# Routed attention with a tanh-shrink MLP: the up-projection of batch 0's second half as seven products of quarters

## Chip, cores, metric

One core of one Trainium2 chip. The metric is device time in microseconds, the median of several runs; a profile is one execution of its own, with a span a little below the run's time.

## The reference

```python
# q, k, v: (4, 8, 768, 64) f32; centroids: (8, 16, 64); w_in: (512, 2048); w_out: (2048, 512)
q_assign = argmax(einsum('bhsd,hcd->bhsc', q_n, c_n), -1)     # *_n: normalized rows
k_assign = argmax(einsum('bhsd,hcd->bhsc', k_n, c_n), -1)
mask = q_assign[:, :, :, None] == k_assign[:, :, None, :]
scores = where(mask, scale * (q @ k.T), -1e9)
attn = softmax(scores); x = attn @ v                          # then (B,H,S,D) -> (B*S, 512)
h = x @ w_in
out = (h - tanh(h)) @ w_out                                   # (3072, 512)
```

A query attends only to keys with its own cluster. The second part is a two-layer MLP over 3072 tokens, 768 for each of the 4 batches.

## The kernel before

**Attention in steps.** Heads go in pairs: 16 pairs, 4 to a batch, numbered n = 0 to 15. A pair is worked in two halves of 384 queries, a half in three steps (NS) of two key blocks: 96 steps in all. HALF is 12 steps. Batch 0 takes all first halves of its pairs (steps 0 to 11), then all second halves (12 to 23); from pair 4 on, a pair's two halves follow each other. The loop over `steps` (its index is `at`) writes out the order on every engine by hand (`manual_schedule`); engines run their lists in that order.

In round `at` the loop issues the scores of step at+1 (`begin`, L451: TensorE matmuls into two PSUM tiles, exponentials by ScalarE), and the values of step `at` (`value`, L505). The masks of step at+1 (`select`, L483: VectorE, exponentials where query and key cluster agree) go into a list `todo`, as do the stages of the next pair's preparation: `turn` transposes (pt, L332), `similar` (sim, L351), `route` (four VectorE operations that find each row's best cluster, L364 to L377), `publish` and `spread` (the codes go through DRAM and come back as a row, L402 and L409). GpSimd adds the masked weights up (L492, L496).

**The MLP between.** A finished batch's MLP is cut into items, and the items due in a round (`now`, chosen by weights that stand for their TensorE time) are placed between the scores and values of that round. Each item calls `between` once or twice, and that issues the next share of `todo`: so masks and items' own evacuations alternate on VectorE. Batch 0's first half is filled into steps 12 to 23, its second half into steps 24 to 47, both by `plain_items`: 16 `up` items (h, L676: 8 matmuls of 384 columns each, tanh on ScalarE, subtraction on VectorE, L683) and 12 `project` items (o, L692). Batches 1 to 3 go by `strassen_items`: seven products of quarters in place of eight, with `up_product` (pu, L871, adds on VectorE L859, tanh L864, subtraction on GpSimd L866) and `down_product` (pd, L922). All three kinds of items share three PSUM buffers (tag "f") with sim, pr, pq and den.

**Factors.** The Strassen weights are sums of quarters of w_in and w_out. `up_maker` and `down_maker` list the work: sums on VectorE (made, L773) into one of three buffers, and writes to DRAM on the SP queue (L737: 28 of 256 KB for w_in; L756: 14 of 512 KB for w_out). These items are handed out in rounds 24 to 45. `fetch_factors` (L795, SP) brings the factors of one block back into one of three stream buffers; `open_stream` gives w_in's place to these buffers in round 39. `right_factors` (L832, VectorE) makes the differences of the quarters of xT, partly in place.

xT of a half is divided by the softmax sums by `divide` (L653, L656) for the last pair of a batch, by `scale` (L638) for others, whose sums take a way through DRAM (`total_both`, `compact`, `invert`, `spread_out`).

Rounds are told by their times in the trace: the scores of steps 21, 22, 23 and 24 begin at 159.8, 170.2, 180.4 and 190.2 us, the first `up` of the second half at 205.8, its first `project` at 290.0, batch 1's first product at 374.6.

Of the kernel before, what the change touches and what calls it, by code (L numbers as in the profile page):

```python
# [39 lines left out]
P = 128  # L40
# [18 lines left out]
def kernel(  # L59
# [119 lines left out]
    def fast():  # L179
# [178 lines left out]
        def route(n: int):  # L358

            t = sims.pop(n)  # L360
            ps = ps_f.tile([P, TB], F32, name="pr", tag="f")
            for j in range(HCH):
                c = slice(j * P, (j + 1) * P)
                nc.tensor.transpose(out=ps[:, c], in_=t[:, c], identity=ident)  # L364
            G = HCH * 8
            pr = ps.rearrange("p (g c) -> p g c", c=C)
            shape = [P, G, C]
            places = down.unsqueeze(1).to_broadcast(shape)
            mx = rtp.tile([P, G], F32, name="mx")
            nc.vector.reduce_max(out=mx, in_=pr, axis=AX.X)  # L370
            top = rtp.tile(shape, F32, name="top")
            nc.vector.tensor_tensor(  # L372
                out=top, in0=pr, in1=mx.unsqueeze(2).to_broadcast(shape), op=ALU.is_ge
            )
            nc.vector.tensor_tensor(out=top, in0=top, in1=places, op=ALU.mult)
            code = codes[n] = codep.tile([P, 2, 2, 2, HCH], F32, name="code")
            nc.vector.reduce_max(  # L377
                out=code.rearrange("p i a h j -> p j (i a h)"),
                in_=top.rearrange("p (j g) c -> p j g c", j=HCH), axis=AX.X,
            )  # L380
# [238 lines left out]
        def spread_out(n: int, half: int):  # L619
            back = lists.pop((n, half))  # L620
            if joined(n):
                pool = late_pools.get("den", sump)
                dens[n, 1] = pool.tile([P, TB], F32, name="den")
                for i in range(2):
                    for h in range(2):
                        nc.sync.dma_start(
                            dens[n, i][h * D : h * D + D], back[i, h : h + 1].to_broadcast([D, TB])
                        )
                return
# [35 lines left out]
        def plain_items(half: int):  # L665
# [39 lines left out]
            if half == 0:  # L705

                order = [(s, i) for i in range(NQ4) for s in range(2)] + order[2 * NQ4 :]
            return [(2.6, 1, lambda between, f=f: up(f, between)) for f in sequence] + [
                (3.4, 1, lambda between, s=s, i=i: project(s, i, between)) for s, i in order
            ]  # L710
# [75 lines left out]
        def fetch_factors(n: int):  # L786

            if n < (B - 1) * PER:
                i = n % PER
                t = streams[n] = late_pools["stream"].tile([P, HF, HM], F32, name="stream")  # L790
# [5 lines left out]

        late_pools, diffs = {}, {}

        def open_stream():
# [3 lines left out]
            )  # L803
            late_pools["den"] = cx.enter_context(
                tc.tile_pool(name="den_late", bufs=1, side="right", reuse_waits="tile")
            )
            for n in range(2):
                fetch_factors(n)

        def open_late():  # L810
            first.close()
            for name, bufs in (
                ("diff", 1), ("u", 2), ("s", 2), ("th", 2), ("g", 1), ("left", 1), ("du", 1),
                ("c", 4), ("raw", 2),
            ):
# [4 lines left out]
            late_pools["S1"] = late_pools["left"].tile([P, HF, TB], F32, name="S1")  # L820

        def right_factors(b: int, c: int):

            if c == 0:
                diffs[b] = late_pools["diff"].tile([P, 3, CH, TB], F32, name="diff")
            d = diffs[b]
            x, y = xT[b * HP + c], xT[b * HP + CH + c]
            for out, u, w in (
# [4 lines left out]

        def strassen_items(b: int):
            base = (b - 1) * PER

            held = {}
            G, left1 = late_pools["G"], late_pools["S1"]

            def up_product(i: int, k_: int, between):  # L840
                which = PRODUCTS[k_]
                x = [xT[b * HP + c] for c in range(CD)]
                d = diffs[b]
                right = {
                    1: [x[c][:, 0] for c in range(CH)], 2: [x[CH + c][:, 0] for c in range(CH)],
                    3: [x[CH + c][:, 1] for c in range(CH)], 4: [d[:, 2, c] for c in range(CH)],
                    5: [d[:, 0, c] for c in range(CH)], 6: [d[:, 1, c] for c in range(CH)],
                    7: [x[c][:, 1] for c in range(CH)],
                }[which]
                if k_ == 0:  # L850
                    held[i] = (
                        late_pools["s"].tile([P, TB], F32, name="s"),
                        late_pools["u"].tile([P, 2, TB], F32, name="u"),
                    )
                s, u = held[i]
                g = G[:, i]

                def add(out, x, y):
                    nc.vector.tensor_tensor(out=out, in0=x, in1=y, op=ALU.add)  # L859

                def shrink(f: int, halves_=slice(0, 2)):
                    t = g[:, f, halves_]
                    th = late_pools["th"].tile([P, 2, TB], F32, name="th")[:, halves_]
                    nc.scalar.activation(out=th, in_=t, func=ACT.Tanh)  # L864
                    t, th = (x.rearrange("p a n -> p (a n)") for x in (t, th))
                    nc.gpsimd.tensor_tensor(out=t, in0=t, in1=th, op=ALU.subtract)  # L866

                ps = ps_f.tile([P, TB], F32, name="pu", tag="f")
                for c in range(CH):
# [7 lines left out]
                elif which == 2:  # L877
                    add(g[:, 0, 0], ps, s)
                    if i == HF - 1:
                        shrink(0, slice(0, 1))  # L880
                elif which == 6:
# [4 lines left out]
                elif which == 4:  # L886
                    add(g[:, 1, 0], ps, u[:, 1])
                elif which == 5:
                    add(u[:, 0], ps, u[:, 0])
                    add(g[:, 1, 1], ps, u[:, 1])  # L890
                    shrink(1)
                else:
                    add(g[:, 0, 1], ps, u[:, 0])

                    shrink(0, slice(1 if i == HF - 1 else 0, 2))
                between()
                if k_ == len(PRODUCTS) - 1:

                    nc.gpsimd.tensor_tensor(out=left1[:, i], in0=g[:, 0, 1], in1=g[:, 1, 1], op=ALU.add)
                    nc.gpsimd.tensor_tensor(  # L900
                        out=g[:, 0, 1], in0=g[:, 0, 0], in1=g[:, 0, 1], op=ALU.subtract
                    )
                    streams.pop(base + i)

            us = {}

            def down_product(k_: int, j: int, between):
# [51 lines left out]

            return [  # L960
                (1.3, 1, lambda between, i=i, k_=k_: up_product(i, k_, between))
                for i in range(HF) for k_ in range(len(PRODUCTS))
            ] + [
                (3.4, 2, lambda between, k_=k_, j=j: down_product(k_, j, between))
# [10 lines left out]
        def before(n: int):  # L975
# [9 lines left out]
            yield lambda: similar(n)  # L985
            yield lambda: route(n)
            yield lambda: publish(n)
# [5 lines left out]

        ready = {}
        for n in range(2, len(pairs)):
# [66 lines left out]
        keep_warm(2)  # L1062
        route(0)
        turn(1, 0, nc.scalar)
        turn(1, 1, nc.scalar)
# [11 lines left out]
        round_piece(rounding.pop(0))  # L1077
        route(1)
        begin(steps[0])
        round_piece(rounding.pop(0))  # L1080
# [22 lines left out]
        for at, (n, half, s) in enumerate(steps):  # L1103
            b, p = pairs[n]
            following = steps[at + 1] if at + 1 < len(steps) else None
            if at == 4 * HALF:
                open_late()
            if at == 4 * HALF - 9:
                open_stream()
            if at in fills:  # L1110
                fill, over = fills[at][0](), fills[at][1]
                whole, spent, since = sum(it[0] for it in fill), 0.0, at
            if at == 2 * HALF:
                makers = [it for i in range(2) for it in up_maker(i)]
                makers += [it for i in range(2) for it in down_maker(i)]
            now = []
# [65 lines left out]
            if following:  # L1182
                todo += [lambda i=i: select(*following[:2], 2 * following[2] + i) for i in range(2)]

                if half == 1 and s == NS - 1 and joined(n):
                    todo.insert(1, lambda n=n: total_both(n))
            todo += [stages[i] for i in (5, 3, 4, 2) if i in stages]
            todo += late
            late = []
# [16 lines left out]

            light = [i for i in range(at, 4 * HALF - 2) if i % 3 and i % 6 != 1]
            if makers and at in light:
# [3 lines left out]
            if "raw" in late_pools:  # L1212
                todo += [check_done, check_done, check_on, check_on]
                if p == HP - 1 and half == 1 and s == NS - 2:
                    todo += [lambda b=b, c=c: right_factors(b, c) for c in range(CH - 1)]
            slots = max(sum(it[1] for it in now), 1)
            place = iter(range(slots))
            turned_at = max(slots - 1 - now[-1][1], 0) if now else 0
# [19 lines left out]
        tail = strassen_items(B - 1)  # L1238

        PRS = len(PRODUCTS)  # L1240
        tail = tail[:2] + tail[PRS : PRS + 2] + tail[2:PRS] + tail[PRS + 2 :]
        for it in tail[:2]:
# [217 lines left out]
```

## Time and profile before

| | us |
|---|---|
| runs | 982.23, 983.19, 982.80 |
| median | 982.8 |
| span of the profiled execution | 981.3 |
| its mean granted TensorE clock | 0.999 |

The profile names a group of instructions by line, engine, operation and tiles (out<-in), then gives shapes, count, busy time, mean duration of one in ns, and the engine's idle time ahead of them with what ended it. In a timeline a row is start, duration, engine, line, operation, shapes and count. In the table by stretch the columns are the stretch, its length, busy time and count for TensorE, its weight loads, VectorE, ScalarE and GpSimd, the clock, the share of DMA and GB/s. In the list of waits: total us, times, longest. DMA-issuing instructions on SP are shown as SPq. Two groups of the kinds that the change moves around:

```profile
L871 PE MATMUL pu<-xT,stream 128*64 128x384 f32 x768 | 134.9, 488 | 0.7 <-DVE top L372 0.7
L683 DVE TENSOR_TENSOR g<-h,th 128x384 f32<-128x384 f32 x32 | 17.6, 551 | 26.4 <-ACT th L681 26.3
```

The first is batches 1 to 3's products on values that are not differences, the second the plain up-projection's evacuation.

### The profile page before, as it was taken

How to read it: one execution, taken by the hardware profiler on the slowest of the kernel's cores; microseconds unless marked ns; L12 is line 12 of the kernel's file. 1: busy time of each engine (PE TensorE's matmuls, PEld its weight loads, DVE VectorE, ACT ScalarE, POOL GpSimd, SP SyncE). 2: the span in 40 equal slices, each digit the busy share in tenths (PEclk: the TensorE clock that was granted, in tenths of full speed). 3: DMA queues.
4: the chain of work that ended last, by engine and by line, in shares of the span. 5: the costliest groups of instructions: out<-in, count | busy, mean ns of one | idle time of the engine just before them, and what ended most of it. 6: DMA issues, size and time to landing. Idle time of an engine off the chain costs nothing.

```text
span 981.3 us, 16550 instructions
## 1 busy us (share of the span) xinstructions
PE 972.3 (99%) x6456; PEld 461.1 (47%) x6456; DVE 534.5 (54%) x1010; ACT 316.6 (32%) x484; POOL 498.8 (51%) x347
## 2 busy tenths in 40 slices
PE   9999999999999999999999999999999999999997
PEld 5433443344443334444455555444455555444664
DVE  6458656447566577647655457655754436543011
ACT  5586554233332333233422222333242121222000
POOL 1026334445445454677686345666688445466600
PEclk9999999999999999999999999999999999999999
DMA  7664452024665633463544646345343132233221
GB/s 201 185 192 142 147 143 94 30 73 132 156 204 166 173 116 110 148 195 99 186 151 158 189 136 201 110 151 149 123 159 135 62 118 95 83 113 129 104 103 35
DMA packets 113385, 132.47 MB, mean 135 GB/s; under 512 B 60388, under 2 KB 93076, under 8 KB 110612
## 3 DMA queue, kind: packets, MB, share of 16 engines
q1 hardware_dynamic: 106916, 109.81, 36.5%
q0 software_dynamic: 6240, 21.50, 6.3%
q8 instruction: 53, 0.87, 0.4%
q14 instruction: 32, 0.26, 0.1%
q10 hardware_dynamic: 144, 0.03, 0.0%
HBM read 110.14 MB, written 21.17 MB: 134 GB/s over the span
## 4 chain that ended last, share of the span: by engine, by line
PE 97%; DVE 1%; DMA 0%; issue 0%; SPq 0%; ACT 0%; DVEq 0%
PE pd L922 22%; PE pu L871 22%; PE sc L451 14%; PE av L505 14%; PE o L692 8%; PE h L676 8%; PE pt L332 2%; PE sim L351 1%; PE den L520 1%; PE warm L302 1%; PE den L566 1%; PE den L539 1%; PE pr L364 1%; DVE e L483 1%; DMA row<-q_codes 0%; PE pq L396 0%
## 5 line engine op out<-in xcount | busy, mean ns | idle before, releaser
L496 POOL TENSOR_TENSOR sum<-sum,e 128x768 f32<-128x768 f32 x112 | 207.2, 1850 | 98.0 <-DVE e L483 92.1
L483 DVE SCALAR_TENSOR_TENSOR e<-row,code,sc 128x384 f32<-128x384 bf16 x336 | 186.2, 607 | 104.2 <-ACT sc L473 89.9
L473 ACT ACTIVATE sc<-sc 128x768 f32<-128x768 f32 x168 | 125.9, 792 | 215.8 <-PE sc L451 206.4
L922 PE MATMUL pd<-stream,G 128*64 128x256 f32 x1728 | 191.5, 379 | 0.0
L922 PEld LDWEIGHTS pd<-stream,G 128*64 128x64 f32 x1728 | 123.7, 137 | 67.0 <-issue 7.7
L451 PE MATMUL sc<-t,t 64*128 64x384 f32 x768 | 150.2, 509 | 0.4 <-ACT e L473 0.3
L505 PE MATMUL av<-e,vals 128*64 128x384 f32 x768 | 145.6, 498 | 0.4 <-DVE e L483 0.4
L871 PE MATMUL pu<-xT,stream 128*64 128x384 f32 x768 | 134.9, 488 | 0.7 <-DVE top L372 0.7
L866 POOL TENSOR_TENSOR G<-G,th 128x768 f32<-128x768 f32 (+1 forms) x51 | 87.3, 1723 | 93.9 <-ACT th L864 93.9
L871 PE MATMUL pu<-diff,stream 128*64 128x384 f32 x576 | 102.3, 488 | 0.0
L451 PEld LDWEIGHTS sc<-t,t 64*128 64x128 f32 x768 | 65.8, 186 | 75.0 <-issue 40.8
L492 POOL TENSOR_TENSOR sum<-e 128x768 f32<-128x768 f32 x28 | 55.5, 1983 | 77.9 <-DVE e L483 42.2
L871 PEld LDWEIGHTS pu<-xT,stream 128*64 128x64 f32 x768 | 54.1, 137 | 69.6 <-issue 61.9
L864 ACT ACTIVATE th<-G 128x768 f32<-128x768 f32 (+1 forms) x51 | 40.9, 806 | 141.2 <-DVE G L859 141.2
L692 PE MATMUL o<-w_out,g 128*64 128x512 f32 x384 | 86.4, 594 | 0.0
L505 PEld LDWEIGHTS av<-e,vals 128*64 128x64 f32 x768 | 47.5, 136 | 82.5 <-issue 79.7
L676 PE MATMUL h<-xT,w_in 128*64 128x384 f32 x512 | 86.3, 487 | 0.0
L871 PEld LDWEIGHTS pu<-diff,stream 128*64 128x64 f32 x576 | 40.4, 137 | 51.0 <-issue 44.7
L859 DVE TENSOR_TENSOR G<-pu,u 128x384 f32<-128x384 f32 x72 | 39.8, 553 | 43.5 <-PE pu L871 43.5
L676 PEld LDWEIGHTS h<-xT,w_in 128*64 128x64 f32 x512 | 36.4, 137 | 46.2 <-issue 45.1
L933 DVE SCALAR_TENSOR_TENSOR c<-pd,du 128x256 f32<-128x256 f32 x36 | 15.2, 421 | 67.0 <-PE pd L922 67.0
L692 PEld LDWEIGHTS o<-w_out,g 128*64 128x64 f32 x384 | 27.0, 137 | 50.1 <-issue 49.4
(131 smaller groups left out, 828.9 us busy)
## 6 DMA issues: line engine op xcount, KB each, us to landing
stream<-up_factors SPq DMA_DIRECT2D x24, 896.0 KB
stream<-down_factors SPq DMA_DIRECT2D x21, 1024.0 KB
raw<-in_moe_w_in_dram POOLq DMA_DIRECT2D x16, 512.0 KB, 4.7
raw<-in_moe_w_out_dram POOLq DMA_DIRECT2D x16, 512.0 KB, 3.9
again<-in_moe_w_in_dram SPq DMA_DIRECT2D x32, 256.0 KB
again<-in_moe_w_out_dram SPq DMA_DIRECT2D x32, 256.0 KB
x<-in_q_dram SPq DMA_DIRECT2D x32, 192.0 KB
x<-in_k_dram SPq DMA_DIRECT2D x32, 192.0 KB
```

The costliest lines, as they stand in the source:

```text
L451: nc.tensor.matmul(sc[i][:, h, 0:TB], lhsT=turned[n, 1][r].rearrange("p a n -> p (a n)")[:, j * P : (j + 1) * P], rhs=turned[n, 0][r, half ...
L473: nc.scalar.activation(out=out, in_=sc[i][:, :, 0:TB], func=ACT.Exp, scale=SCALE)
L483: nc.vector.scalar_tensor_tensor(out=e[:, h], in0=rows[n, half][:, h], scalar=codes[n][:, 1, j // HCH, h, j % HCH : j % HCH + 1], in1=sc[: ...
L492: nc.gpsimd.tensor_tensor(out=s, in0=pair[0], in1=pair[1], op=ALU.add)
L496: nc.gpsimd.tensor_tensor(out=s, in0=s, in1=pair[i], op=ALU.add)
L505: nc.tensor.matmul(avs[n, half][h * D : h * D + D], lhsT=vals[n][:, h, j], rhs=e[i][:, h], start=(j == 0), stop=(j == NCH - 1),)
L676: nc.tensor.matmul(h[r], lhsT=w_in[i][:, c, o * P : (o + 1) * P][:, r], rhs=xT[c][:, half], start=(c == 0), stop=(c == CD - 1),)
L692: nc.tensor.matmul(acc[sub][r], lhsT=gs[f % HF][:, f // HF, sub * P : (sub + 1) * P][:, r], rhs=w_out[f // FQ][:, f % FQ], start=(f == seq ...
L864: nc.scalar.activation(out=th, in_=t, func=ACT.Tanh)
L866: nc.gpsimd.tensor_tensor(out=t, in0=t, in1=th, op=ALU.subtract)
L871: nc.tensor.matmul(ps[r], lhsT=streams[base + i][:, c, k_, r], rhs=right[c], start=(c == 0), stop=(c == CH - 1),)
L922: nc.tensor.matmul(ps[r], lhsT=left(i)[:, r], rhs=t[:, i], start=(i == 0), stop=(i == HF - 1))
```

## The change

The second half of batch 0 takes its up-projection by `up_items`, which is the old `up_product` loop with the batch's places passed in: 8 blocks of 7 products, on quarters of 192 columns for batch 0 (the half's 384 queries are cut in two). Products 1 and 2 of the first two blocks come first. The projections stay `project`.

- The up factors are made in rounds 20 to 22 and the stream is opened in round 23, its first two loads being issued there. The factors are fetched 8 blocks more than before. The down factors are made in rounds 36 to 46.
- The differences are made at the start of round 24's items, ahead of the masks of step 25.
- In rounds 24 to 35 the masks of the next step are issued ahead of the round's items (with `total_both` between them where it is due); `route` is cut in two there, and its last two VectorE operations (`route_on`) come later in the list.
- The weights of items: 0.65 for a product, 3.0 for a projection of this half.
- Scratch for s and u, and for one denominators' tile, is taken from the pool of turned q and k.

```diff
+        def route_on(n: int):
+            top = tops.pop(n)
             nc.vector.tensor_tensor(out=top, in0=top, in1=places, op=ALU.mult)
             code = codes[n] = codep.tile([P, 2, 2, 2, HCH], F32, name="code")
             nc.vector.reduce_max(
...
+            ups = [(2.6, 1, lambda between, f=f: up(f, between)) for f in sequence]
+            if half == 1:
+                ups = half_up_items(gs)
+            return ups + [
+                (3.4 if half == 0 else 3.0, 1, lambda between, s=s, i=i: project(s, i, between)) for s, i in order
             ]
...
-                i = n % PER
+                i = n + HF if n < 0 else n % PER
...
+            half_pools["diff"] = mid.enter_context(
+                tc.tile_pool(name="diff_mid", bufs=1, side="right", reuse_waits="tile")
             )
             for n in range(2):
-                fetch_factors(n)
+                fetch_factors(n - HF)
...
+        def columns(b: int, c: int):
+            return xT[b * HP + c] if b else xT[c][:, 1].rearrange("p (a n) -> p a n", a=2)
...
-            x, y = xT[b * HP + c], xT[b * HP + CH + c]
+            x, y = columns(b, c), columns(b, CH + c)
...
-        def strassen_items(b: int):
-            base = (b - 1) * PER
+        def up_items(b: int, base: int, quarter, shrink, done):
             held = {}
+            width = TB if b else TB // 2
...
-                ps = ps_f.tile([P, TB], F32, name="pu", tag="f")
+                ps = ps_f.tile([P, TB], F32, name="pu", tag="f")[:, 0:width]
...
+        def start_without(items):
+            n = len(PRODUCTS)
+            return items[:2] + items[n : n + 2] + items[2:n] + items[n + 2 :]
+
+        def half_up_items(gs):
+            W = TB // 2
+            def quarter(i: int, f: int, t: int):
+                if i not in gs:
+                    gs[i] = gp.tile([P, 2, TB], F32, name="g")
+                return gs[i][:, f, t * W : (t + 1) * W]
+            def shrink(i: int, f: int, parts):
+                cols = slice(parts.start * W, parts.stop * W)
+                t = gs[i][:, f, cols]
+                th = thp.tile([P, TB], F32, name="th")[:, cols]
+                nc.scalar.activation(out=th, in_=t, func=ACT.Tanh)
+                nc.gpsimd.tensor_tensor(out=t, in0=t, in1=th, op=ALU.subtract)
+            return start_without(up_items(0, -HF, quarter, shrink, lambda i: None))
...
-            if at == 4 * HALF - 9:
+            if at == 2 * HALF - 1:
                 open_stream()
...
+            if at == 2 * HALF - 4:
+                makers = [it for i in range(2) for it in up_maker(i)]
             if at == 2 * HALF:
-                makers = [it for i in range(2) for it in up_maker(i)]
-                makers += [it for i in range(2) for it in down_maker(i)]
+                makers = [it for i in range(2) for it in down_maker(i)]
...
-            light = [i for i in range(at, 4 * HALF - 2) if i % 3 and i % 6 != 1]
+            light = [i for i in range(max(at, 3 * HALF), 4 * HALF - 1) if i % 6 != 1]
+            if at < 2 * HALF - 1:
+                light = list(range(at, 2 * HALF - 1))
...
+            if at == 2 * HALF:
+                for c in range(CH):
+                    right_factors(0, c)
+            if 2 * HALF <= at < 3 * HALF:
+                masks = 3 if half == 1 and s == NS - 1 else 2
+                for it in todo[:masks]:
+                    it()
+                todo = todo[masks:]
```

## The prediction

> **What bounds the kernel now.** I read the busy table and the waits of TensorE first, because they decide whether removed matmuls are removed time; then the timeline around the place of the edit; then the DMA by stretch. The page's first part, its clock row, and the three longest entries of TensorE's wait list:
>
> ```profile
> PE 972.3 (99%) x6456; PEld 461.1 (47%) x6456; DVE 534.5 (54%) x1010; ACT 316.6 (32%) x484; POOL 498.8 (51%) x347
> ...
> PEclk9999999999999999999999999999999999999999
> ```
> ```profile
> PE warm L302 <- DVE inverses L231: 1.3, 1, 1.3
> PE pu L871 <- DVE top L372: 0.7, 2, 0.3
> PE av L505 <- DVE e L483: 0.4, 1, 0.4
> ```
>
> TensorE is busy from end to end at full clock, and all its listed waits come to 2.9 us. So every microsecond of matmul taken out in the middle is a microsecond of span, as long as no wait is put in its place. The question is then twofold: what the products cost on TensorE, and whether anything that feeds them comes late.
>
> The matmul's price must be read from starts, since 486 ns records overlap. From the timeline of TensorE (start, duration, instructions at the end; each f32 matmul is two instructions):
>
> ```profile
> 377.24 1.46 PE L871 MATMUL pu<-diff,stream 128*64 128x384 f32 x8
> 378.53 1.46 PE L871 MATMUL pu<-xT,stream 128*64 128x384 f32 x8
> ...
> 491.27 7.08 PE L922 MATMUL pd<-stream,G 128*64 128x256 f32 x64
> 498.27 1.56 PE L451 MATMUL sc<-t,t 64*128 64x384 f32 x8
> ...
> 501.10 3.62 PE L922 MATMUL pd<-stream,G 128*64 128x256 f32 x32
> 504.66 0.55 PE L364 MATMUL pr<-ident,simt 128*128 128x128 f32 x3
> ```
>
> Eight instructions of 384 columns take 378.53 - 377.24 = 1.29 us, 161 ns each. For 256 columns, 64 take 7.00 and 32 take 3.56, so 32 more cost 3.44, 107.5 ns each. That is 0.42 ns a column plus about 1 ns, and a change of product inside a run costs nothing. 192 columns should take 81.3 ns (estimate from these two).
>
> **What the Trainium skill says.** "TensorE: Matmul & The Clock Gate", section Back-to-back issue gap, gives N/2.4 + 2.5 ns warm: 82.5 ns for 192 columns, close to my 81.3. It warns that loads of weights also pace small matmuls; its section on LDWEIGHTS prices a load by its columns, P/1.2 ns, 53 ns for 64. The trace has no 192-column matmul; it shows a pair of 64-column loads lying over each other in about 140 ns, while a pair of 192-column matmuls would take 163. "DMA: Bandwidth & Descriptors", section Queues, rings and completion order, says descriptors of one issuing engine are consumed in ring order on each DMA engine: the new stream loads stand behind the factor writes of the same queue. "GPSIMD Engine Reference", section Specifications, says POOL contends with VectorE instructions of two SBUF inputs. The trace agrees: scaling xT (two SBUF inputs) has a mean of 1420 ns at 384 columns, while the adds of L859, with one input in PSUM, stay at 553 to 555.
>
> **The change part by part.**
>
> ```profile
> L676 PE MATMUL h<-xT,w_in 128*64 128x384 f32 x512 | 86.3, 487 | 0.0
> L866 POOL TENSOR_TENSOR G<-G,th 128x384 f32<-128x384 f32 x6 | 6.0, 1004 | 4.8 <-ACT th L864 4.8
> L496 POOL TENSOR_TENSOR sum<-sum,e 128x768 f32<-128x768 f32 x112 | 207.2, 1850 | 98.0 <-DVE e L483 92.1
> ```
>
> Removed: half of L676, 256 instructions x 161.3 ns = 41.3 us of TensorE. Added: 8 blocks x 7 products x 2 row blocks x 2 column halves = 224 matmuls, 448 instructions x 81.3 ns = 36.4 us. Difference -4.9 us. The number of runs, each with some 0.1 us at its edge, stays about the same (12 steps with one run each), so I take 0 there. The 12 output projections keep their matmuls; only their place shifts by fractions of a step.
>
> The differences: 8 VectorE operations of 192 columns. 128 columns cost 294 ns and 384 cost 553, so about 360 ns, 2.9 us in all; with contention up to 1.2 us more. They follow the last scaling of xT:
>
> ```profile
> 198.16 0.56 DVE L656 TENSOR_TENSOR xT<-xT,den 128x384 f32<-128x384 f32 x1
> 206.16 2.19 DVE L483 SCALAR_TENSOR_TENSOR e<-row,code,sc 128x384 f32<-128x384 bf16 x4 [7.45 <-ACT sc L473]
> ```
>
> VectorE idles 7.45 us there; the differences fit. The first product that needs one is the fifth, and it starts at about 205.8 + 4 x 0.65 = 208.4. Cost 0.
>
> Evacuation: 64 adds of 192 columns (0.36 us) instead of 16 subtractions (0.55): 23 against 8.8 us, over twelve steps of about 6.2 us, next to 2.2 us of masks a step. VectorE has 54 of 79 us busy in this stretch before (205.8 to 284.6), partly the sums for the factors, which move away. ScalarE gains 8 short copies. GpSimd gains 17 subtractions of 384 columns at 1.0 us beside 24 sums at 1.85: 61 of about 74 us. The sums have two steps until their weight buffer is wanted again, so I put this at 0.
>
> What does reach TensorE is the order masks, then adds. In a step that begins at 0, scores end at 1.5, values at 2.8, products follow every 0.65. In the trace masks start 1.91 us after the scores (208.55 to 210.46) and four take 2.2: the first add ends at about 4.45. Three PSUM buffers make the fourth product, at 4.8, wait for it: a margin of 0.3. It fails where route_on's two operations come first (one step, some 0.3 us) and where a route's transposes share the buffers with five products (one step, 0.4). I charge 0.8 us, between 0 and 5 (0.4 in each step).
>
> The factors and their transfer. In the trace the 28 writes of 256 KB are issued from 201.8 to 280.0; now they lie in the three steps from about 167, and the loads of blocks 0 and 1 are issued behind them on SP. Four such writes, then the DMA over time:
>
> ```profile
> 223.28 0.91 SPq L737 DMA_DIRECT2D up_factors<-made  x2
> 224.23 1.33 SPq L737 DMA_DIRECT2D up_factors<-w_in  x2
> ```
> ```profile
> 224.00:228.00 4.00, 4.00 (x26) 1.63 (x24) 2.95 (x6) 1.14 (x2) 3.88 (x2) 1.00 0.91 262
> ...
> 168.00:198.00 30.00, 30.00 (x152) 10.90 (x149) 14.20 (x22) 6.66 (x10) 14.10 (x10) 1.00 0.09 28
> ```
>
> 0.91 of 4 us for four: 0.91 us each. The stretch from 168 to 198 is empty before (share 0.09). The twelve first writes are done by 182. The other sixteen are released by VectorE's fourth factor, made after the xT scaling that ends at 180.3, and go out from about 182.6: 16 x 0.91 = 14.6, other transfers 1.6, two loads of 896 KB at 326 GB/s (308 to 318) 5.6, landing 0.7. Block 0 lands at about 202.3, block 1 at 205.1; they are wanted at 205.8 and 207.1. Cost 0, at worst 3 us, since the margin is only 2. The queue SP also holds the row of masks for step 24 between these writes (about 184.5, wanted at 192.1) and the next pair's q and k behind the loads, wanted twenty and more us later. VectorE waits for a write before reusing one of three buffers, but the masks behind it slip by at most 1.7 us (from 182.2), where the scores' PSUM is wanted at 190.2. Later, the other factors' work is one operation a step, and one of 1.2 to 1.6 us lies ahead of step 48's masks; the slack there is 2 us.
>
> Sum: -4.9 + 0.8 = -4.1 us; 981.3 becomes 977.2 in the profiled span. The other runs are 982.2 to 983.2, median 982.8, so **978.7 us**.
>
> **The rivals.** (A) The adds become the bound: masks first leaves 0.3 us of margin, and 0.4 us lost in each of twelve steps is 4.8 us, 982.7, no change. For: three PSUM buffers, twice and more VectorE work on products. Against: the strassen stage of batch 1 alternates masks and adds with only 0.7 us of waits on TensorE. (B) The other side: the writes come late. Place: block 1's load, at 207.1. From 182.6 + 16w + 7.9 the decision falls at w = 1.04 us a write; at 1.3 the gain is gone, at 1.5 TensorE stands still 7.4 us and the run takes about 986. For: nothing in the trace shows sixteen writes back to back with VectorE and SP both waiting for them. Against: 262 to 285 GB/s in the stretches that are full. (C) Weight loads pace the products: if two loads do not overlap further than now and a pair of products takes 214 ns as at 256 columns, 224 x 0.214 = 47.9 us instead of 36.4, 990. For: no 192-column row. Against: the transposes pt take 1.46 us for 12, 113 to 122 ns each, with 128-column loads of 141 ns, so such loads overlap.
>
> **How the numbers follow.** The forecast 0.72 (977 to 980.7), A 0.14, B 0.09, C 0.05. A measurement of this kernel tells about 0.2%, 2 us, from no change. Faster: the forecast and a part of A, 0.76; same: the rest of A and the milder B, 0.14; slower: B and C, 0.10. The range reaches down to the sum with no stall at all, 977.9, less 1.0 for the spread of the runs, 976.9, and up to 982.2, which takes in most of A and a mild B.
>
> **What would show it.** 448 instructions of 192 columns, 0.65 us between products in a run; TensorE's list without a wait on the stream and with less than 1.5 us on VectorE's adds; first product at about 205.8, second half's work from there to the first score of batch 1's stage about 4 us shorter. Wrong would be: an idle stretch before the first or third product that ends with a DMA; the fourth product of each step waiting for VectorE; or products 0.8 us and more apart.

## The result, and the profile after

| | before | after |
|---|---|---|
| median of six runs each, us | 982.7 | 979.39 (979.27 to 979.54) |
| ratio after / before | | 0.9966, 95% interval 0.9953 to 0.9979 |
| span of the profiled execution, us | 981.3 | 977.6 |

3.3 us less in the runs, 3.7 us in the profiled spans, where 4.1 had been forecast. The six executions of the changed kernel spanned 977.5 to 977.8 us; five more of it, run beside the experiments, spanned 977.1 to 978.4. So half a microsecond between two profiles says nothing by itself.

The busy table and the clock row of the page, and four groups of instructions by line and shape (busy us, mean ns):

```profile
PE 968.4 (99%) x6648; PEld 474.3 (49%) x6648; DVE 549.4 (56%) x1058; ACT 318.2 (33%) x493; POOL 514.4 (53%) x364
...
PEclk9999999999999999999999999999999999999999
```
```profile
L684 PE MATMUL h<-xT,w_in 128*64 128x384 f32 x256 | 42.9, 487 | 0.0
L887 PE MATMUL pu<-xT,stream 128*64 128x192 f32 x256 | 24.7, 329 | 0.0
L887 PE MATMUL pu<-diff,stream 128*64 128x192 f32 x192 | 18.9, 329 | 0.0
L882 DVE TENSOR_TENSOR g<-pu,t 128x192 f32<-128x192 f32 x32 | 11.1, 353 | 7.2 <-PE pu L887 5.7 <-ACT t L892 1.0
```

TensorE is as full as before. The 256 matmul instructions of 384 columns are gone, 448 of 192 columns have come, and the adds take 0.35 us each, as estimated. Busy time can't say what an instruction of 192 columns costs, since records overlap (329 ns each). The timeline of TensorE can, from starts:

```profile
205.84 2.82 PE L887 MATMUL pu<-xT,stream 128*64 128x192 f32 x32
208.71 0.87 PE L887 MATMUL pu<-diff,stream 128*64 128x192 f32 x8
209.51 1.56 PE L456 MATMUL sc<-t,t 64*128 64x384 f32 x8
...
218.50 0.82 PE L887 MATMUL pu<-diff,stream 128*64 128x192 f32 x8
219.15 0.82 PE L887 MATMUL pu<-xT,stream 128*64 128x192 f32 x8
```

From 218.50 to 219.15 is one product: 0.65 us for eight instructions, 81.25 ns each. In the first step four products should take 2.60 us, but the fifth starts 2.87 us after the first: a wait of 0.27 us that the list of waits doesn't show, because the ends of matmuls are modelled. It ends with VectorE's first add, which stands behind the masks (208.30 to 208.65).

The first product starts at 205.84, where the first matmul of the plain up-projection stood before (205.81). The first projection of this half then starts at 286.26 instead of 290.00, batch 1's first product at 370.86 instead of 374.61. So the gain of 3.7 us arises between the first product and the first projection, and nothing is gained or lost after that. The two ends of this stretch before, and the later one after:

```profile
205.81 2.80 PE L676 MATMUL h<-xT,w_in 128*64 128x384 f32 x16
...
290.00 1.51 PE L692 MATMUL o<-w_out,g 128*64 128x512 f32 x6
```
```profile
286.26 1.08 PE L700 MATMUL o<-w_out,g 128*64 128x512 f32 x4
```

Where within that stretch is a sum of rows, a row being products (or plain `up` matmuls) until another kind of matmul starts. The edge of a row is what it takes beyond its instructions. Before there are 12 rows, 42.59 us: 256 x 161.25 ns = 41.28, and 1.31 at the edges, 0.11 a row. After there are **16 rows**, 38.74 us: 448 x 81.25 ns = 36.40, 0.54 of waits (0.32 in the first row, 0.22 in that of 253.56, by what these two take beyond the 0.10 of rows like them), and 1.80 at the edges, again 0.11 a row. The rows differ by 3.85.

### The profile page after: what moved, and what is told of

Same layout as the page of the kernel before. It is cut to its first block, busy times and chain, and to the rows that moved or that the text cites. A ratio compares the mean times of both kernels' runs of the same rounds, so it can differ in the third digit from the quotient of the medians.

```text
span 977.6 us, 17050 instructions
## 1 busy us (share of the span) xinstructions
PE 968.4 (99%) x6648; PEld 474.3 (49%) x6648; DVE 549.4 (56%) x1058; ACT 318.2 (33%) x493; POOL 514.4 (53%) x364
## 4 chain that ended last, share of the span: by engine, by line
PE 96%; DMA 1%; DVE 1%; issue 0%; ACT 0%; SPq 0%; DVEq 0%
PE pu L887 26%; PE pd L983 22%; PE av L510 14%; PE sc L456 14%; PE o L700 9%; PE h L684 4%; PE pt L332 2%; PE sim L351 1%; PE warm L302 1%; PE den L525 1%; PE den L571 1%; PE den L544 1%; PE pr L364 1%; DMA hot<-q_codes 1%; DVE e L488 1%; DMA q_codes<-qc 0%
## 5 line engine op out<-in xcount | busy, mean ns | idle before, releaser
L887 PE MATMUL pu<-xT,stream 128*64 128x384 f32 (+1 forms) x1024 | 159.6, 448 | 0.7 <-DVE top L371 0.7
L887 PE MATMUL pu<-diff,stream 128*64 128x384 f32 (+1 forms) x768 | 121.2, 448 | 0.0
L887 PEld LDWEIGHTS pu<-xT,stream 128*64 128x64 f32 x1024 | 72.0, 137 | 74.6 <-issue 64.6
L497 POOL TENSOR_TENSOR sum<-e 128x768 f32<-128x768 f32 x28 | 52.7, 1880 | 58.5 <-DVE e L488 36.4
L887 PEld LDWEIGHTS pu<-diff,stream 128*64 128x64 f32 x768 | 53.7, 137 | 56.2 <-issue 46.6
L994 DVE SCALAR_TENSOR_TENSOR du<-pd,du 128x256 f32<-128x256 f32 x27 | 11.4, 420 | 60.4 <-PE pd L983 60.4
L684 PE MATMUL h<-xT,w_in 128*64 128x384 f32 x256 | 42.9, 487 | 0.0
```

Source lines behind the costliest of these rows:

```text
L497: nc.gpsimd.tensor_tensor(out=s, in0=pair[0], in1=pair[1], op=ALU.add)
L684: nc.tensor.matmul(h[r], lhsT=w_in[i][:, c, o * P : (o + 1) * P][:, r], rhs=xT[c][:, half], start=(c == 0), stop=(c == CD - 1),)
L887: nc.tensor.matmul(ps[r], lhsT=streams[base + i][:, c, k_, r], rhs=right[c], start=(c == 0), stop=(c == CH - 1),)
```

## The experiments

Spans are compared with 977.6 and 977.9 of the changed kernel; the medians with the kernel before on the same chip.

**All but the products.** The change with its second half's up-projection left plain (a projection's weight is 3.4 again):

```diff
-            if half == 1:
-                ups = half_up_items(gs)
...
-                fetch_factors(n - HF)
+                fetch_factors(n)
...
-            if at == 2 * HALF - 1:
+            if at == 4 * HALF - 9:
                 open_stream()
...
-                    right_factors(0, c)
```

> Everything the change moves is kept (up factors made in rounds 20 to 22, the masks ahead of the round's items, route cut in two), but the second half's up-projection stays plain: 256 instructions of 384 columns, no products, no differences, the stream opened in round 39. Nothing is left out of the computation. My theory, that the gain is TensorE time of the products alone (38.7 us of stretches against 42.6): no gain is left, the span is that of the kernel before, 981.3 us, give or take 0.5. Rival, that the new order of masks or the emptier stretch later gives part of the gain: a span of 978 to 980.5. Rival on the other side, that the early factors cost something which the products' gain covered: over 982.

Span 981.7, median 983.42 against 983.28 of the kernel before, ratio 1.0003 (0.9995 to 1.0012). Early factors, masks ahead and the cut route give nothing by themselves, and what they take is too small for the times: the stretch from the first `up` to the first projection is 84.77 us (205.50 to 290.27) against 84.19 before. 0.4 of these 0.6 us lie in the rows of `up`, of which there are 14 here: with the masks ahead, route's transposes fall between two `up` items at two places. The gain is that of the products.

**Masks shared out between the products.** The lines that issue the masks ahead of the items are taken out:

```diff
-            if 2 * HALF <= at < 3 * HALF:
-                masks = 3 if half == 1 and s == NS - 1 else 2
-                for it in todo[:masks]:
-                    it()
-                todo = todo[masks:]
```

> The changed kernel, but in rounds 24 to 35 the masks of the next step are again shared out between the products instead of ahead of them. Nothing is left out. Theory of the scores' buffers: the scores have two buffers; with the masks shared out, the second mask stands behind the last product's add and ends about 1.5 us after it, while the second scores of the next step could start 0.75 us after it. A wait of 0.3 to 0.9 us in most of twelve steps: 3 to 9 us, a span of 981 to 987. The view of the prediction, where masks ahead of the adds are only a charge on the products (0.8 us): without it the span falls by about 0.5, to 977.1.

Span 990.7, ratio to the kernel before 1.0094 (1.0077 to 1.0111): slower than before. 0.5 of the 13.1 us stands ahead of the stretch. TensorE's list of waits (us in total, times, longest) and a place in its timeline:

```profile
PE sc L456 <- DVE e L488: 5.1, 11, 0.9
PE pt L332 <- ACT t L339: 2.2, 2, 1.1
...
PE av L510 <- DVE e L488: 1.1, 3, 0.4
```
```profile
208.97 0.82 PE L887 MATMUL pu<-diff,stream 128*64 128x192 f32 x8
209.72 0.92 PE L456 MATMUL sc<-t,t 64*128 64x384 f32 x4
211.33 0.92 PE L456 MATMUL sc<-t,t 64*128 64x384 f32 x4 [0.69 <-DVE e L488]
```

The second four score matmuls start 1.61 us after the first four instead of 0.75: their buffer is read by a mask that stands behind the last product's add. Waits in this stretch add up to 8.7 us more than in the changed kernel, and TensorE's busy time is 3.9 longer, where modelled ends cover waits. The transposes of `turn` (pt) use the scores' buffers too and then have only one of the two. The direction was expected, the size not: 12.6 instead of 3 to 9, since every kind of matmul that uses those buffers waits, and values (av) as well. The products need this order: without it the change is a loss of 9 us.

**More writes ahead of the stream.** Eight of the factor writes are issued twice:

```diff
-                for c in range(CH):
+                for c in [*range(CH)] * (2 if which in (3, 6) else 1):
                     nc.sync.dma_start(
```

> The changed kernel, but 8 of the 28 writes of up factors (the sums 6 and 3) are issued twice, with the same contents: 8 more writes of 256 KB ahead of the first two loads of the stream on the same queue. Nothing is left out. Theory of the prediction (a write takes 0.91 us, margins of 3.5 us for block 0 and 2.0 for block 1): the loads land 7.3 us later, TensorE stands still 5.3 us in all before the products of block 1, span 982.9. With the margins that the trace after suggests (block 0 landing near 202, block 1 near 204.2): 4.4 us, span 982. Rival, that the transfers hide in any case, because TensorE's start is set by something else: 977.6. Rival, that the writes are slower when queued so (1.3 us each): over 985.

Span 984.7 in its one execution, 7.1 more. First the issue of the stream's first two loads on SP, in the changed kernel and then in this one; then this one's wait on TensorE, a wait of its SP queue, and its clock (the third number from the end) by stretch:

```profile
196.91 1.69 SPq L807 DMA_DIRECT2D stream<-up_factors  x2
```
```profile
206.34 1.02 SPq L807 DMA_DIRECT2D stream<-up_factors  x2
211.66 4.32 PE L887 MATMUL pu<-xT,stream 128*64 128x192 f32 x32 [5.85 <-DMA stream<-up_factors]
```
```profile
SPq L749 <- DMA up_factors<-made: 10.5, 8, 2.9
```
```profile
211.60:213.00 1.40, 1.34 (x10) 1.01 (x11) 0.00 (x0) 0.00 (x0) 0.00 (x0) 0.50 0.97 398
213.00:214.40 1.40, 1.40 (x12) 1.05 (x10) 0.00 (x0) 0.32 (x1) 0.00 (x0) 0.50 1.21 271
214.40:215.80 1.40, 1.40 (x18) 1.18 (x16) 0.36 (x1) 0.32 (x1) 0.00 (x0) 0.87 1.36 220
```

The loads go out 9.43 us later, and TensorE stands still 5.9 us. So 9.4 - 5.9 = 3.5 us of margin was there. The same figures from the other end: block 0 arrives 5.3 us after its issue; if it takes as long in the changed kernel, it is there at 196.91 + 5.3 = 202.2, and the product wants it at 205.84. The margin was sized right.

The delay is no price of a write, though 9.43 / 8 = 1.18 us looks like one. Each repeat goes to the place of the write before it and waits on SP until that one has landed, 10.5 us in eight waits that the changed kernel doesn't have. What a write takes in its queue is read from the changed kernel: its last fourteen are issued from 183.25 to 196.91, with a row of masks of 0.90 between them, so 0.91 us each, as the prediction had it.

The remaining 1.2 us is a surprise: after the pause the granted clock is 0.50 until about 214.8, and the first row takes 4.90 us instead of 3.67.

**The differences behind the masks.**

```diff
-            if at == 2 * HALF:
-                for c in range(CH):
-                    right_factors(0, c)
...
                 todo = todo[masks:]
+            if at == 2 * HALF:
+                for c in range(CH):
+                    right_factors(0, c)
```

> The changed kernel, but the eight differences stand behind the masks of step 25 on VectorE instead of in the idle time ahead of them. Nothing is left out. Theory: they cost nothing only because of that idle time. Behind the masks they take 208.3 to 211.3, the adds of the first products stand behind them, and the fourth product waits for the first add until about 211.7 instead of 207.8: TensorE loses 3.7 us that nothing gives back, span 981.3. Rival, that VectorE's slack in this step absorbs them: under 978.2.

Span 984.3, ratio 1.0018 (1.0008 to 1.0028), slower than before; 0.5 of the 6.7 us lies ahead of the place. The profile is the longest of nine executions. They span 981.5 to 984.3, 983.3 in the median, which is some 5.5 us more than the changed kernel's, and their mean clocks go from 0.999 in the shortest to 0.996, so the pause doesn't cost the same each time. The timeline of TensorE, three of the differences, and the clock by stretch:

```profile
206.34 2.82 PE L887 MATMUL pu<-xT,stream 128*64 128x192 f32 x32
212.04 0.91 PE L887 MATMUL pu<-diff,stream 128*64 128x192 f32 x4 [2.87 <-DVE diff L853]
213.14 0.91 PE L887 MATMUL pu<-diff,stream 128*64 128x192 f32 x4 [0.20 <-DVE diff L853]
213.98 2.93 PE L456 MATMUL sc<-t,t 64*128 64x384 f32 x8
216.84 2.31 PE L510 MATMUL av<-e,vals 128*64 128x384 f32 x8
```
```profile
208.80 1.22 DVE L853 TENSOR_TENSOR diff<-xT 128x192 f32<-128x192 f32 x1
210.05 1.84 DVE L853 TENSOR_TENSOR diff<-xT,diff 128x192 f32<-128x192 f32 x1
211.82 0.34 DVE L853 TENSOR_TENSOR xT<-xT 128x192 f32<-128x192 f32 x1
```
```profile
212.00:214.00 2.00, 1.77 (x10) 0.64 (x10) 1.97 (x8) 0.00 (x0) 0.00 (x0) 0.50 0.03 8
214.00:215.50 1.50, 1.50 (x8) 0.90 (x8) 0.46 (x2) 0.00 (x0) 0.00 (x0) 0.50 0.02 5
215.50:217.00 1.50, 1.50 (x8) 0.42 (x6) 0.37 (x1) 0.80 (x1) 0.00 (x0) 0.50 0.00 0
```

The wait is there, but at the fifth product, which needs the differences, and not at the fourth: the fourth reuses the buffer of product 1, which ScalarE copies out (L892), so no VectorE add stands before it. Some 2.4 us of the wait are not the differences' own time: the first two start while GpSimd works on two sums (207.99 to 211.68) and take 1.22 and 1.84, the other six 0.34 to 0.36. The scores that take 1.49 us elsewhere take 2.86 here, at half clock. The rest beyond the wait comes from there, which the next run tests.

**The same with TensorE kept busy.**

```diff
-                for c in range(CH):
+                again = 5 if b == 0 and i == 1 and which == 2 else 1
+                for c in [*range(CH)] * again:
```

> As the run with the differences behind the masks, but the fourth product of the first step is worked five times over into the same buffer (four times 0.65 us of TensorE, with the same result), so that TensorE is busy while the differences are made. The run without it lost 3.1 us in the wait and, by the traces, some 2.2 us more because the granted clock stood at 0.50 for about 5 us afterwards. Theory, that the pause brought the clock down: here the clock stays at 1.00 and only 3.1 us are lost (2.6 of repeats, 0.5 of wait), a span of 980.7 to 981.2. Rival, that the low clock was there for another reason: about 984, as without the repeats.

Span 981.0. The clock in two of the same stretches:

```profile
212.00:214.00 2.00, 1.44 (x11) 0.89 (x12) 1.83 (x7) 0.00 (x0) 0.00 (x0) 1.00 0.03 8
214.00:215.50 1.50, 1.50 (x10) 0.48 (x8) 0.55 (x2) 1.44 (x2) 0.00 (x0) 1.00 0.00 0
```

The clock stays at 1.00, scores and values take 2.84 us as in the changed kernel, and from the scores of step 25 to the first product of the next step TensorE loses 3.6 us against the 6.2 without repeats. Work of no use made the program 3.3 us shorter by these two profiles, and about 2 us by the medians (983.03 against 985.09): the pause brought the clock down.

**Half of each product left out.**

```diff
-                for c in range(CH):
+                depth = CH if b else CH // 2
+                for c in range(depth):
```

> The changed kernel with half of each product of the second half's up-projection left out (only the first of its two terms over the contraction): 224 matmul instructions of 192 columns fewer, with all masks, adds and transfers kept. If TensorE alone bounds the stretch: 224 x 81.3 ns = 18.2 us less, a span of 959.4. By the prediction's model of masks first (adds begin 4.45 us into a step, three buffers): in a step of five half products the fourth starts at 4.45 instead of 3.98 and the fifth at 4.8, so some 0.5 us a step is lost, 6 us in all: 965.5. If the adds bound the stretch already in the changed kernel: 975 or more.

Span 969.6 in its one execution: 8.0 to 8.3 us less, where the removed instructions are worth 18.2. Its list of waits and a place in its timeline:

```profile
PE pu L888 <- DVE t L882: 2.8, 4, 1.3
PE pu L888 <- DVE g L882: 1.7, 3, 0.8
...
PE pu L888 <- DVE top L371: 1.2, 3, 0.6
```
```profile
217.36 0.50 PE L888 MATMUL pu<-diff,stream 128*64 128x192 f32 x4
219.19 0.55 PE L888 MATMUL pu<-diff,stream 128*64 128x192 f32 x4 [1.34 <-DVE t L882]
```

Products wait for adds that stand behind the masks. About 10 us are lost, 0.8 a step, more than the 0.5 of the model; 6.3 of them stand in the list of waits of this stretch, 0.7 of these on ScalarE. TensorE bounds the changed kernel, but VectorE's adds are near: more than half of this further cut went to waits.

**Rows of products not cut.** Route's and turn's transposes after the last product, and in round 24 the masks behind the second product's add:

```diff
-                    todo.append(lambda: route_on(routed.pop()))
+                    after = [todo.pop(), lambda: route_on(routed.pop())]
...
+            if 2 * HALF <= at < 3 * HALF:
+                turned_at = slots - 1
...
+                while i == 1 and lead:
+                    lead.pop(0)()
...
+            for it in after:
+                it()
```

> The changed kernel with three moves in rounds 24 to 35, nothing left out: the transposes of route (pr) and of turn (pt) stand after the last product of the round instead of between two products, and in round 24 the masks stand behind the second product's add. Theory, that each change of kind inside a row of products costs TensorE about 0.11 us: four runs of products fewer, 0.45 us; and the wait of 0.27 us before the first product on differences and that of 0.22 behind route's second operation at 253.6 go too: 0.9 us in all, a span of 976.7. Rival, that route's four operations now stand ahead of the masks of the next step and push its first adds back by 0.5 us twice: the gain is lost, 977.2 to 978.

Span 979.1, median 980.99, ratio 0.9982 (0.9973 to 0.9990): it loses 1.2 to 1.5 us on the changed kernel. There are two new waits of 0.60 and 0.64 us of a product on an add. Joining a row at `turn` saves nothing: values after transposes take 1.44 us instead of 1.39, as much as is saved in the row. Two runs take the moves apart.

**Route whole again.**

```diff
-                if at < 2 * HALF or at >= 3 * HALF:
+                if True:
                     stage = todo.pop()
```

> The changed kernel, but route is not cut in two in rounds 24 to 35: as a single item of the list it then stands after the last product of its round, with all four of its VectorE operations ahead of the next step's masks. Nothing is left out. Theory, from the run with joined rows of products (a wait of 0.60 us in step 27 and of 0.64 in the second step of this kind, both on an add that stands behind the masks): the loss is route's place and nothing else, +1.2 us of waits less 0.3 for two rows of products that are no longer cut, a span of 978.5 to 978.9. Rival, that the loss there came from the moves of turn or of the first step's masks: 977.3 to 977.9.

Span 978.0, ratio 0.9970 (0.9958 to 0.9982): no difference from the changed kernel that the times can tell, and less loss than expected. The stretch from the first product to the first projection takes 81.00 us, against 80.42 in the changed kernel and 81.82 with joined rows. The edit brings route's transposes behind the last product at one of their two places only; at the other they still stand between two products (254.07). There is one wait, of 0.32 us, in place of 0.60. The cause shows in one VectorE operation, route's product of two tiles in SBUF, in the changed kernel, in this one, and in the one with joined rows, in the last two with a GpSimd subtraction ahead of it:

```profile
216.19 0.64 DVE L380 TENSOR_TENSOR top<-top,down 128x384 f32<-128x384 f32 x1
```
```profile
216.31 1.00 POOL L942 TENSOR_TENSOR g<-g,th 128x384 f32<-128x384 f32 x1
216.75 0.97 DVE L380 TENSOR_TENSOR top<-top,down 128x384 f32<-128x384 f32 x1
```
```profile
216.76 0.99 POOL L942 TENSOR_TENSOR g<-g,th 128x384 f32<-128x384 f32 x1
216.91 1.25 DVE L380 TENSOR_TENSOR top<-top,down 128x384 f32<-128x384 f32 x1
```

Each time it starts while GpSimd works and ends 0.41 us after that instruction has ended: a sum that ends at 216.41 in the changed kernel, the subtractions that end at 217.31 and 217.75 in the moved orders, where the masks wait behind it. The changed kernel pays at the other place: 1.12 us there, against 0.68 with route whole and 1.22 with joined rows; before it was 0.56 at both. So cutting route in two is worth at most 0.6 us here, and the joined version's loss is this stretched operation with several small shifts on top; how much falls to each wasn't separated.

**The first step's masks.** Only that move:

```diff
+                lead, todo = todo[:masks], todo[masks:]
+                if at > 2 * HALF:
+                    while lead:
+                        lead.pop(0)()
...
+                while i == 1 and lead:
+                    lead.pop(0)()
```

> The changed kernel, but in round 24 alone the masks stand behind the second product's add instead of ahead of all adds. Nothing is left out. Theory: the wait of 0.2 to 0.27 us ahead of the first product on differences goes, the second scores of the next step may wait 0.1: a span of 977.4 to 977.8, no difference that the times can tell. Rival, that the later masks push the adds of the next step back: over 978.2.

Span 978.0, median 979.21, ratio 0.9960 (0.9946 to 0.9973). The first row takes 3.40 us instead of 3.67, the scores behind it 1.60 instead of 1.49, so 0.16 is gained at the place itself; the span differs by what lies ahead of it. The wait is explained, and it is too small for the times. No version tried beats the changed kernel by more than they can tell.

The kernel itself was run once more beside these:

> The changed kernel itself, as the measure for the other runs of this set: a span of 977.6 us, some 0.5 either way, which is also how far spans of one kernel may differ.

Span 977.9, ratio 0.9964 (0.9950 to 0.9977).

## Why the prediction was right

- **TensorE bounds.** Right. Without the products the rest of the change is worth nothing (1.0003), and what TensorE saves in the rows of products, 3.85 us, arrives in the span as 3.7. Rival A, the adds as the bound, didn't occur, but it is near: of 18.2 us of matmuls taken out, 10 came back, nearly all of the listed ones as waits on VectorE. The adds are 56 and not the 64 that the prediction counts (seven to a block), 19.6 us instead of 23.
- **The price of the products.** Right: 81.25 ns against 81.3, so -4.9 us. Rival C, weight loads that pace the products, would have needed 0.86 us a product; they take 0.65. The working to 81.3 isn't clean: the two prices it names, 161 ns for 384 columns and 107.5 for 256, lie on a line without a constant, which gives 80.6 for 192. The "about 1 ns" doesn't come out of them; that the sum met the measured price within 0.1 us is luck, though the error would only have been 0.3 us.
- **"The number of runs, each with some 0.1 us at its edge, stays about the same (12 steps with one run each), so I take 0 there."** This step failed, by the count and not by the price of an edge. The transposes of route and turn fall between products, and 12 rows became 16: 1.80 us of edges instead of 1.31, 0.5 more. In the plain order they stood at the end of a row. Both parts of the change move them: in the run without products, where the masks alone were ahead, route's two cut a row (14 rows), and in the run with products and the masks shared out, all four do (16 rows).
- **Masks ahead of the adds, 0.8 us (0 to 5).** The size was about right (0.54), the places only in part. Of its two places, the step of five products with route's transposes has a wait, 0.22 us instead of 0.4: the third product of the row of 253.56 starts at 255.03, when VectorE has read the transposes' buffer (L371, until 254.89). Where `route_on` comes first the row has none, and it takes four operations ahead of the masks to make one (0.32 us). The first step's 0.32 wasn't foreseen. What the prediction didn't see is what this order is worth: it was treated as a charge alone, and leaving it out costs 12.6 us. That batch 1's stage alternates masks and adds with little waiting was put forward against rival A; that stage is no evidence for products half as long.
- **The differences at nothing.** Right, and because of the idle time named. The timeline of VectorE in the changed kernel:

```profile
198.67 1.17 DVE L853 TENSOR_TENSOR diff<-xT 128x192 f32<-128x192 f32 x1
199.87 0.36 DVE L853 TENSOR_TENSOR diff<-xT,diff 128x192 f32<-128x192 f32 x1
...
201.61 0.35 DVE L853 TENSOR_TENSOR diff<-xT,diff 128x192 f32<-128x192 f32 x1
206.19 1.14 DVE L488 SCALAR_TENSOR_TENSOR e<-row,code,sc 128x384 f32<-128x384 bf16 x2 [4.23 <-ACT sc L478]
```

  Seven take 0.35 and one 1.17; they are done at 202.0, and the masks start at 206.19 as before (206.16). The first starts beside a GpSimd operation (198.24 to 199.62). Behind the masks their step lost 6.2 us in the profile with the slow clock and 3.6 in that with TensorE kept busy.
- **The transfer at nothing, margin 3.5 us for block 0.** Right: 202.2 by the delay measured in the run with eight more writes, against 202.3; no run measured the 0.7 us of landing by itself. Rival B didn't occur: the writes went out at 0.91 us each, below the 1.04 from which B was to decide. But a late load would have cost more than B had it, since a pause costs the slow clock as well: 7.1 us for 5.9 of pause in that run.

The working with measured terms is -4.88 for the instructions, +0.49 for edges, +0.54 for waits: -3.85. The prediction had -4.9 + 0.8 = -4.1. That it came so near is in part luck: a term of 0.5 put at nothing stands beside a charge that was 0.3 too high.

## What to carry to other kernels

Price a replacement of matmuls from starts in the timeline, and then count the rows that the new items make, because each change of kind on TensorE took about 0.1 us here. Smaller items can turn a harmless order on another engine into the bound: look which buffers that engine frees (here the scores', read by the masks), and serve that one first. A cost put at nothing is as good as the margin that hides it; state the margin, and put a pause of TensorE as long as the two here (3.1 and 5.9 us) at more than its length. And look what GpSimd does when an operation on two SBUF tiles starts on VectorE: in these traces it waited for GpSimd's instruction to end.

## What the runs showed of the hardware

In two profiles a pause of TensorE brought its granted clock down. The Trainium skill, "TensorE: Matmul & The Clock Gate", section "What's actually happening", says the array falls to half speed after an idle window of about 3.4 us and comes back after a busy one of about that length. The runs agree in kind, not in each number. The clock (third from the end) around its fall and its return, with eight more writes and then with the differences late:

```profile
207.00:208.00 1.00, 0.00 (x0) 0.00 (x0) 1.00 (x3) 0.00 (x0) 0.62 (x1) 0.96 0.90 237
214.00:215.00 1.00, 1.00 (x10) 0.79 (x8) 0.36 (x1) 0.00 (x0) 0.00 (x0) 0.62 1.34 236
```
```profile
209.00:212.00 3.00, 0.17 (x3) 0.00 (x0) 2.97 (x3) 0.00 (x0) 2.60 (x2) 0.95 0.79 301
217.00:219.00 2.00, 2.00 (x10) 0.76 (x12) 1.90 (x4) 0.80 (x1) 1.09 (x1) 0.62 0.00 0
```

By these shares it falls to half at about 207.9 and 211.7 and returns at about 214.8 and 218.5: 6.8 us of half clock both times. It falls 2.2 and 2.7 us after the last matmul before the pause (205.74 and 208.94, from starts), so sooner than the page's window. And what slows TensorE is the part of the 6.8 us that is left when it starts again: 3.1 us after the pause of 5.9, 6.5 us after that of 3.1 (208.94 to 212.04). The shorter pause left more half clock behind it. A pause of 1.5 us in the run with half products left the clock at 1.00.

A VectorE operation on two SBUF tiles waited for GpSimd. "GPSIMD Engine Reference", section Specifications, names this contention; the traces price it. In the profile of the changed kernel, from 100 us on, 26 of the xT scalings, differences and route's products started while a GpSimd addition or subtraction ran. 25 of them ended 0.41 to 0.42 us (384 columns) or 0.22 us (192) after that instruction had ended, whatever its length, and took up to 2.17 us; the other 46 took 0.54 to 0.56 and 0.35 to 0.36. The profile before has the same, 22 of 23. So such an operation takes what is left of GpSimd's instruction when it starts and 0.41 or 0.22 us more, and an order that moves it by half a microsecond can change its price by as much.
